# First blocks of a mixture of experts in plain fp32 for four experts, in place of split fp32r products for five

## The chip, the cores and the metric

The kernel runs on one core of one Trainium2 chip. Times are device microseconds (us) of whole executions; the profile is one further execution, with the start and end of the instructions on each engine: PE (TensorE matmuls) and PEld (its weight loads), DVE (VectorE), ACT (ScalarE), POOL (GpSimd) and SP, whose queue issues most of the DMAs.

## The reference

Attention over a window of 128 keys, for 8 batches, 8 heads, 576 positions and 64 columns a head; its output is a matrix x of 4608 tokens by 512. Then a mixture of 8 experts: each token goes to the best two by a noisy gate.

```python
logits = x @ w_gate
noise_scale = np.log1p(np.exp(x @ w_noise))
noisy_logits = logits + noise_scale * noise
top2 = np.argpartition(-noisy_logits, 2, axis=1)[:, :2]
...
for e in range(E):
    for k in range(2):
        mask = top2[:, k] == e
        ...
        h = np.maximum(x[mask] @ w1[e], 0.0)
        out[mask] += top2_w[mask, k, None] * (h @ w2[e])
```

w1[e] is 512 by 1024 and w2[e] 1024 by 512, so an expert is two chained products with a ReLU between them.

## The kernel before, in words

**Attention** runs over 32 pairs of heads, in three groups of query blocks each: scores (L455, and L448 for the last 64 positions, once a pair), softmax on DVE and ACT, transposes (L492), the product with the values (L523). For each batch of 576 tokens `rows` turns the result to token rows (L632, L635) and `gate` gets the logits (L655, L666); then `route(b)` chooses two experts for each token of batch b. `route` is a chain of some fifty small DVE operations with two stops on PE: counts over the tokens (L723 to L727, called R below) and the list of token numbers by expert (L770, called H below). `listed` (L777) takes the list from PSUM, and a POOL scatter (L843) adds it to `slots` in DRAM. Route b + 1 can't start its own chain before route b has gone through; the eight are numbered 0 to 7.

**First blocks.** When two batches are routed (`CUTS`), the first 256 tokens of each of the first NF = 5 experts are already known. Their experts' products (`first`, 5 blocks of 256 tokens) fill PE while attention goes on. A block has 8 steps f, one for every 128 of the 1024 inner columns. A step is `mm1` (L1086), which makes 128 inner columns for 256 tokens from four 128-row pieces of w1, then `middle` (ReLU, L1108 or L1110), then `mm2` (L1136), which adds to two 128 x 512 tiles of the output. The operands are fp32 numbers cut in a high and a low part of type fp32r, and each product is made as three: high by high, high by low, low by high. The low parts cost operations: for the weights a copy and a subtraction (`weight`, L960 to L962, the subtraction on POOL or DVE), for the tokens L1079, for the inner columns L1125. Tiles of this stage have names with `a`: `axh`, `axl`, `ahh`, `ahl`, `w1ha`, `w1la`, `w2ha`, `w2la`. Raw weights come into `raw1` and `raw2` (three buffers each), the parts into 5 sets (`wsets`).

**Second blocks.** When attention and all routes are over, `second_wave` gives the freed memory to new tiles (names with `b`), and all the other tokens go through the experts one after another, with f16 parts and again three products: blocks of 512 and 448 tokens for the experts that had a first block, of 512, 384 and 320 for the others (`BLOCKS`); CAP = 1216 tokens is the most of an expert that this takes. `mm2_flipped` (L1141) is the second product of an expert's last block. Tokens come by a POOL gather (L1034), are scaled (`fit`, L1051), transposed on PE (L1066) and split (L1076). `size_of_weights` reads the next expert's weights a second time (`mraw`) to find the scale of its f16 parts.

**Order.** The program is written by a small list scheduler (`Order`): each operation has a rank, and an engine that is free takes the ready operation of lowest rank, with durations that the code gives. What results is a fixed order for each engine, in which an instruction that waits holds up all behind it. `FFN0` and `FFN1` spread the ranks of the first blocks' steps; with fewer steps the distance between two steps grows. `named[0, NF - 1, 7]` is the point from which the second blocks' weights may be loaded.

## Time and profile before

| | |
|---|---|
| time, median of 3 runs | 1215.79 us (1214.66 to 1219.39) |
| the profiled execution | 1212.61 us |
| its span, from the first to the last instruction | 1210.7 us |
| mean granted TensorE clock | 0.988 |
| instructions | 20898 |

How to read it: busy times are sums of the spans of an engine's instructions, and the idle time in front of a group is put down to what ended it. Matmuls run in a pipeline, so one lasts longer than the distance to the next one; rates are read from the distance of their starts. The 40 slices of the page show three parts:

```profile
PE   7998899999997889999999999999999999999995
DVE  6798787788898897664664674584563473373310
POOL 5000121231255661320330331233033320332211
```

Each digit is the busy share of 30 us in tenths. PE is near its full share nearly everywhere; the dip in the 12th to 15th slice is the passage from attention to the second blocks, and there DVE and POOL are busiest.

### The profile page before, as it was taken

What the parts mean: (1) busy time and instruction counts of PE and PEld (TensorE: products, weight loads), DVE (VectorE), ACT (ScalarE), POOL (GpSimd) and SP (SyncE); (2) the same over time, 40 slices, a digit from 0 to 9 for tenths busy, and PEclk for the clock granted to TensorE, in tenths of its full rate; (3) what the DMA queues carried; (4) which work ended last, traced back from release to release, by engine and by line L of the source; (5) the groups of instructions that cost most, each with busy time, mean ns of one, the idle gap of its engine ahead of it and who ended that gap; (6) DMA issues with size and microseconds to landing.
All of it is one profiled execution on the core that took longest, in us unless ns stands there. A gap on an engine that the chain in (4) does not pass through costs nothing.

```text
span 1210.7 us, 20898 instructions
## 1 busy us (share of the span) xinstructions
PE 1142.3 (94%) x7336; PEld 690.1 (57%) x7336; DVE 775.9 (64%) x2483; ACT 547.3 (45%) x1378; POOL 310.7 (26%) x343
## 2 busy tenths in 40 slices
PE   7998899999997889999999999999999999999995
PEld 4666677777776764554544544545545654575552
DVE  6798787788898897664664674584563473373310
ACT  8776666667633353441432433342432441252311
POOL 5000121231255661320330331233033320332211
PEclk9999999999999999999999999999999999999998
DMA  8896545553267597562761862663663391352221
GB/s 289 281 319 208 172 130 172 161 151 125 77 184 179 125 280 217 134 186 91 178 187 45 206 171 54 186 191 58 193 166 62 80 264 41 62 114 45 35 27 23
DMA packets 138987, 177.57 MB, mean 147 GB/s; under 512 B 25728, under 2 KB 89472, under 8 KB 138880
## 3 DMA queue, kind: packets, MB, share of 16 engines
q1 hardware_dynamic: 120960, 135.87, 35.3%
q0 software_dynamic: 17920, 40.33, 17.5%
q8 instruction: 59, 0.97, 0.3%
q14 instruction: 48, 0.39, 0.1%
HBM read 134.76 MB, written 41.40 MB: 146 GB/s over the span
## 4 chain that ended last, share of the span: by engine, by line
PE 58%; DVE 13%; DMA 8%; issue 4%; POOL 1%; ACT 0%; SPq 0%; POOLq 0%; another core or an unknown queue 0%; DVEq 0%
PE bank L1086 23%; PE bank L1136 16%; PE bank L1141 8%; DMA mraw<-in_w_dram 5%; PE bank L523 2%; PE bank L492 2%; DMA xg<-xs_dram,ix 2%; DVE wam L988 2%; PE bank L1066 2%; PE bank L455 2%; DVE hot L765 1%; POOL out_dram L1215 1%; DVE bxl L1076 1%; DVE fit L1051 1%; DMA raw<-in_w_dram 1%
## 5 line engine op out<-in xcount | busy, mean ns | idle before, releaser
L1125 DVE SCALAR_TENSOR_TENSOR bhl<-bank,bhh 128x512 f16<-128x512 f32 (+3 forms) x152 | 93.9, 618 | 282.9 <-ACT bhh L1108 282.7
L1215 POOL DMA_INDIRECT out_dram<-yo,ix x70 | 110.3, 1575 | 534.3 <-ACT yo L245 480.4
L1108 ACT ACTIVATE bhh<-bank 128x512 f16<-128x512 f32 (+3 forms) x143 | 77.7, 543 | 332.8 <-PE bank L1086 331.9
L1086 PE MATMUL bank<-bxh,w1hb 128*128 128x512 f16 (+3 forms) x608 | 213.5, 351 | 0.0
L1086 PE MATMUL bank<-bxl,w1hb 128*128 128x512 f16 (+3 forms) x608 | 213.4, 351 | 0.0
L1086 PE MATMUL bank<-bxh,w1lb 128*128 128x512 f16 (+3 forms) x608 | 213.4, 351 | 0.0
L1086 PEld LDWEIGHTS <-w1hb 128*128 128x128 f16 x1216 | 118.0, 98 | 104.8 <-issue 1.9
L480 ACT ACTIVATE p<-p,nm 128x256 f32<-128x256 f32 (+2 forms) x288 | 133.8, 469 | 8.5 <-DVE nm L473 8.4
L1136 PE MATMUL bank<-w2hb,bhl 128*128 128x512 f16 (+1 forms) x352 | 133.5, 379 | 4.2 <-DVE bhl L1125 4.2
L1136 PE MATMUL bank<-w2hb,bhh 128*128 128x512 f16 (+1 forms) x352 | 133.7, 380 | 0.6 <-ACT bhh L1108 0.5
L1136 PE MATMUL bank<-w2lb,bhh 128*128 128x512 f16 (+1 forms) x352 | 133.4, 379 | 0.0
L1136 PEld LDWEIGHTS <-bhh 128*128 128x128 f16 (+1 forms) x704 | 67.3, 98 | 72.9 <-issue 4.6
L473 DVE CUSTOM_DVE_ANT_0 p<-bank,bias 128x256 f32<-128x256 f32 (+2 forms) x288 | 95.5, 380 | 17.4 <-PE bank L455 15.8
L1086 PEld LDWEIGHTS <-w1lb 128*128 128x128 f16 x608 | 59.5, 98 | 54.7
L962 POOL TENSOR_TENSOR w1la<-raw,w1ha 128x512 fp32r<-128x512 f32 x35 | 48.7, 1392 | 161.9 <-ACT w1ha L245 115.2
L523 PE MATMUL bank<-pT,vraw 128*64 128x128 f32 (+3 forms) x896 | 81.2, 303 | 5.6 <-ACT p L480 3.3
L492 PE MATMUL bank<-ident,p 128*128 128x128 f32 x512 | 83.2, 287 | 1.6 <-DVE pT L249 0.7
L1034 POOL DMA_INDIRECT xg<-xs_dram,ix x70 | 70.0, 1000 | 43.0 <-issue 37.9
L988 DVE TENSOR_REDUCE wam<-mraw 128x1 f32<-128x1024 f32 x56 | 67.7, 1211 | 19.9 <-DMA mraw<-in_w_dram 19.6
L455 PE MATMUL bank<-qk 64*128 64x256 f32 (+1 forms) x512 | 70.7, 389 | 10.2 <-DVE nm L473 5.3
L1141 PE MATMUL bank<-bhl,w2hb 128*128 128x448 f16 (+1 forms) x224 | 75.5, 337 | 0.0
L1141 PE MATMUL bank<-bhh,w2lb 128*128 128x448 f16 (+1 forms) x224 | 75.5, 337 | 0.0
(219 smaller groups left out, 2119.9 us busy)
## 6 DMA issues: line engine op xcount, KB each, us to landing
raw<-in_w_dram SPq DMA_DIRECT2D x208, 256.0 KB, 3.9
mraw<-in_w_dram SPq DMA_DIRECT2D x56, 512.0 KB, 6.6
qk<-in_qk_dram SPq DMA_DIRECT2D x32, 608.0 KB, 4.5
out_dram<-xg SPq DMA_DIRECT2D x10, 1024.0 KB, 8.6
vraw<-in_v_dram SPq DMA_DIRECT2D x16, 512.0 KB, 3.9
xs_dram<-x SPq DMA_DIRECT2D x32, 256.0 KB, 3.4
vraw<-in_v_dram SPq DMA_DIRECT2D x16, 128.0 KB, 5.5
xg<-xs_dram,ix POOLq DMA_INDIRECT x70, 4.8
```

The lines of the kernel that those rows point to most:

```text
L455: nc.tensor.matmul(s[h][:, o:o + c], qk[half, i * 128:i * 128 + 128], qk[half, QW + k0:QW + k0 + c], start=True, stop=True)
L473: nc.vector.tensor_tensor_reduce(out=p[:, z, h, 0:c], in0=s[h][:, o:o + c], in1=bv, scale=-0.125, scalar=3.0e38, op0=OP.add, op1=OP.min, a ...
L480: nc.scalar.activation(pv, pv, AF.Exp, bias=nm[:, z, h:h + 1], scale=-1.0, accum_out=den[:, z, 2 * g + h:2 * g + h + 1])
L492: nc.tensor.transpose(t[:, z], p[:, h, a:a + 128], ident)
L523: nc.tensor.matmul(o[half, o0:o0 + c], t[p0:128, kb, hh:hh + D], w, start=m == 0, stop=m == len(lst) - 1)
L988: yield dve(1.13, rank, lambda: nc.vector.tensor_reduce(o, t, axis=AX.X, op=OP.max, apply_absolute_value=True))
L1086: nc.tensor.matmul(t[:, 0:blk.n], wp[:, c], x[:, c, 0:blk.n], start=c == 0 and z == 0, stop=c == 3 and z == 2)
L1108: nc.scalar.activation(o, i, AF.Relu)
L1125: yield dve(0.07 + c * 0.00104, rank - MIDDLE, lambda: nc.vector.scalar_tensor_tensor(hl[:, 0:c], t[:, 0:c], 0.0, high, op0=OP.max, op1=OP ...
L1136: nc.tensor.matmul(blk.y[j][0:r], h[:, cs], wp, start=f == 0 and m == 0, stop=f == 7 and m == 2)
L1141: nc.tensor.matmul(blk.y[c][:, 0:blk.n], wp[:, c * 128:c * 128 + 128], h[:, 0:blk.n], start=f == 0 and m == 0, stop=f == 7 and m == 2)
L1215: ins = nc.gpsimd.indirect_dma_start(out=out, out_offset=bass.IndirectOffsetOnAxis(ap=blk.ix[0:r, j:j + 1], axis=0), in_=t[0:r], in_offset ...
```

## The change

The first blocks' products are made once, as fp32 matmuls on the raw weights and the raw tokens. The low parts of weights, tokens and inner columns, the copies and the subtractions that made them, and their tiles are gone; a weight is loaded straight into one of 8 sets (2 tiles each, not 4), and the three `hh` buffers were two. NF is 4: expert 4 has no first block, and its second blocks are those of 512, 384 and 320 tokens. The scheduler's durations for the two products are changed with them; the ranks' constants are as they were.

```diff
-NF = 5
+NF = 4
...
-    wsets = [Ring([weight_set(keep, F32R, f"a{z}") for z in range(5)]), Ring([])]
+    wsets = [Ring([(keep.tile([128, 4, 128], F32, name=f"w1a{z}"), keep.tile([128, DM], F32, name=f"w2a{z}"))
+                   for z in range(8)]), Ring([])]
...
-    rings1 = block_rings(keep, FIRST[0], F32R, "a", 2)
+    rings1 = block_rings(keep, FIRST[0], F32, "a", 3)
...
+                if p == 0:
+                    w = ev[2] = yield (wsets[p], r)
+                    mark(named[p, e, f])
+                    for z, src in enumerate((first_weight(e, f), second_weight(e, f))):
+                        spawn(weight(w[z], ev[z], r + 0.2 * z, src, e, z, f))
+                    continue
                 a = yield (raw1, r)
                 b = yield (raw2, r)
                 w = yield (wsets[p], r)
...
-    def weight(t, r, hi, lo, ev, rank, src, e, z, f):
+    def weight(t, ev, rank, src, e, z, f):
         yield from move(2.6e5, rank, lambda: nc.sync.dma_start(t, src))
-        yield either(0.52, 0.34, rank, LATE[5], lambda g: copy(g, hi, t))
-        yield Op((("POOL", 1.23, rank), ("DVE", 0.6, rank + WEIGHTS_LATE)),
-                 lambda g: engine[g].tensor_sub(lo, t, hi.bitcast(F32)))
-        put(r, t)
         mark(ev)
...
+        hi = blk.xh[:, :, cs]
+        yield either(0.48, 0.6, rank, LATE[6], lambda e: copy(e, hi, tv))
         if blk in second:
-            yield either(0.48, 0.6, rank, LATE[6], lambda e: copy(e, hi, tv))
-            yield dve(0.6, rank, lambda: nc.vector.tensor_sub(lo, tv, hi))
-        else:
-            yield either(0.48, 0.6, rank, LATE[6], lambda e: copy(e, hi, tv))
-            yield dve(0.6, rank, lambda: nc.vector.tensor_sub(lo, tv, hi.bitcast(F32)))
+            yield dve(0.6, rank, lambda: nc.vector.tensor_sub(blk.xl[:, :, cs], tv, hi))
...
     def mm1(blk, t, w, cc):
         for c in cc:
+            if blk not in second:
+                nc.tensor.matmul(t[:, 0:blk.n], w[0][:, c], blk.xh[:, c, 0:blk.n], start=c == 0, stop=c == 3)
+                continue
...
-            us = 3 * (blk.n / 2400 + (0.005 if p else 0.016))
+            us = 3 * (blk.n / 2400 + 0.005) if p else blk.n / 600
...
-        yield dve(0.07 + c * 0.00104, rank - MIDDLE, lambda: nc.vector.scalar_tensor_tensor(
-            hl[:, 0:c], t[:, 0:c], 0.0, high, op0=OP.max, op1=OP.subtract))
+        if blk in second:
+            yield dve(0.07 + c * 0.00104, rank - MIDDLE, lambda: nc.vector.scalar_tensor_tensor(
+                hl[:, 0:c], t[:, 0:c], 0.0, hh[:, 0:c], op0=OP.max, op1=OP.subtract))
...
     def mm2(blk, f, j, r, w):
         cs = slice(j * 128, j * 128 + r)
+        if blk not in second:
+            nc.tensor.matmul(blk.y[j][0:r], blk.h[f][1][0][:, cs], w[1], start=f == 0, stop=f == 7)
+            return
...
-                end = yield pe(0.655 if p else 0.69, rank, lambda: mm2(blk, f, j, r, ev[2]), False)
+                end = yield pe(0.655 if p else 0.86, rank, lambda: mm2(blk, f, j, r, ev[2]), False)
```

What this does to the order is seen in three places. First PE, right behind the last list H (route 7). Before, a step's products come in threes (`w1ha` and `w1la` are parts of one weight, `axh` and `axl` of the tokens; the number behind a name is the buffer):

```order
L1136 MATMUL bank_70<-w2ha_176,ahh_211 128x512
L1136 MATMUL bank_70<-w2la_177,ahh_211 128x512
L1136 MATMUL bank_70<-w2ha_176,ahl_213 128x512
L1136 MATMUL bank_72<-w2ha_176,ahh_211 128x512
L1136 MATMUL bank_72<-w2la_177,ahh_211 128x512
L1136 MATMUL bank_72<-w2ha_176,ahl_213 128x512
L1086 MATMUL bank_66<-axh_208,w1ha_178 128x256
L1086 MATMUL bank_66<-axl_210,w1ha_178 128x256
L1086 MATMUL bank_66<-axh_208,w1la_179 128x256
```

The changed kernel has at the same place (its L1085 is `mm1`, L1139 `mm2`, L1068 the transposes of the second blocks' tokens):

```order
L1139 MATMUL bank_70<-w2a_179,ahh_207 128x512
L1139 MATMUL bank_73<-w2a_179,ahh_207 128x512
L1085 MATMUL bank_67<-axh_204,w1a_180 128x256 x2
L1085 MATMUL bank_71<-axh_204,w1a_182 128x256
L1068 MATMUL bank_68<-ident,xg_121 128x128 x4
L1139 MATMUL bank_70<-w2a_181,ahh_205 128x512
L1139 MATMUL bank_73<-w2a_181,ahh_205 128x512
L1085 MATMUL bank_71<-axh_204,w1a_182 128x256 x3
```

One matmul stands for three. Counted over the whole order: when L448 comes for the 32nd and last time, 15 of 40 steps of `mm1` are behind it before, and 12.25 of 32 now; between the R of routes 6 and 7 there are 9.5 steps before and 4.25 now, between the last H and the first transpose of second tokens 6 and 4.75.

Second DVE, in route 7, from `u` (L710) to the largest logits (L715, MAX). Before:

```order
L710 TENSOR_SCALAR u<-y 128x40
L249 CAST w2ha_184<-raw_118 128x512
L247 TENSOR_SCALAR yo_206<-bank_68,gw_201 128x512
L782 SCALAR_TENSOR_TENSOR y<-u,y 128x40
L783 RECIPROCAL u<-u 128x40
L784 TENSOR_TENSOR y<-y,u 128x40
L785 TENSOR_TENSOR l<-l,y 128x40
L962 TENSOR_TENSOR w1la_183<-raw_115,w1ha_182 128x512
L787 SCALAR_TENSOR_TENSOR l<-lg_152,l 128x40
L788 TENSOR_TENSOR l<-l,noi 128x40
L789 TENSOR_TENSOR l<-l,lg_152 128x40
L1079 TENSOR_TENSOR axl_209<-bank_73,axh_207 128x4x128
```

Now (line numbers are lower by one there):

```order
L709 TENSOR_SCALAR u<-y 128x40
L781 SCALAR_TENSOR_TENSOR y<-u,y 128x40
L782 RECIPROCAL u<-u 128x40
L783 TENSOR_TENSOR y<-y,u 128x40
L784 TENSOR_TENSOR l<-l,y 128x40
L786 SCALAR_TENSOR_TENSOR l<-lg_152,l 128x40
L787 TENSOR_TENSOR l<-l,noi 128x40
L788 TENSOR_TENSOR l<-l,lg_152 128x40
L714 MAX tp<-l 128x8 x5
```

Everything that belonged to the first blocks has left the chain, and stays out of it to the end of route 7.

Third POOL, around the last scatter of a list. Before (L1317 is a small table, L1215 the scatter of a first block's output rows):

```order
L962 TENSOR_TENSOR w1la_183<-raw_117,w1ha_182 128x512
L962 TENSOR_TENSOR w1la_187<-raw_115,w1ha_186 128x512
L842 MEMSET pad 1x1
L843 DMA slots_dram<-listed,line_of_147 704x64
L1317 IOTA bias 1x80
L962 TENSOR_TENSOR w1la_191<-raw_116,w1ha_190 128x512
L962 TENSOR_TENSOR w2la_193<-raw_119,w2ha_192 128x512
```

Now, behind the same scatter (L842) and the table, up to the first gathers of second tokens (L1222 is the scatter of output rows, L1036 the gather):

```order
L1222 DMA out_dram<-yo_201,ids_172 5120x512
L1221 MEMSET pad 1x1
L1222 DMA out_dram<-yo_202,ids_172 5120x512
L1036 DMA xg_121<-xs_dram,ix_4062 128x520
L1036 DMA xg_122<-xs_dram,ix_4062 128x520
```

No subtraction is left on POOL; two scatters of a first block's output still stand between the last list and the first gather.

More of the change, by code (lines that the diff above doesn't have):

```diff
@@ L9 @@
 F32 = mybir.dt.float32
-F32R = mybir.dt.float32r
 F16 = mybir.dt.float16
@@ L898, in block_rings @@
     def block_rings(pool_, c, dt, name, hn):
-        return {"xh": ring(pool_, 2, [128, 4, c], dt, name + "xh"), "xl": ring(pool_, 2, [128, 4, c], dt, name + "xl"),
-                "hh": ring(pool_, hn, [128, c], dt, name + "hh"), "hl": ring(pool_, hn, [128, c], dt, name + "hl")}
-    wsets = [Ring([weight_set(keep, F32R, f"a{z}") for z in range(5)]), Ring([])]
+        return {r: ring(pool_, 2 if r[0] == "x" else hn, [128, 4, c] if r[0] == "x" else [128, c], dt, name + r)
+                for r in (("xh", "hh") if dt == F32 else ("xh", "xl", "hh", "hl"))}
+    wsets = [Ring([(keep.tile([128, 4, 128], F32, name=f"w1a{z}"), keep.tile([128, DM], F32, name=f"w2a{z}"))
+                   for z in range(8)]), Ring([])]
     wam = keep.tile([128, 2, 2, 8], F32, name="wam")
@@ L946, in weights @@
                 for z, (t, rg, src) in enumerate(((a, raw1, first_weight(e, f)), (b, raw2, second_weight(e, f)))):
-                    make = weight if p == 0 else scaled_weight
-                    spawn(make(t, rg, w[2 * z], w[2 * z + 1], ev[z], r + 0.2 * z, src, e, z, f))
+                    spawn(scaled_weight(t, rg, w[2 * z], w[2 * z + 1], ev[z], r + 0.2 * z, src, e, z, f))
     def first_weight(e, f):
@@ L966, in weight @@
             yield dve(0.6, rank + SIZES[0], lambda: nc.vector.tensor_reduce(
-                wam[:, e % 2, z, f:f + 1], hi.bitcast(F32), axis=AX.XY if z == 0 else AX.X, op=OP.max,
-                apply_absolute_value=True))
+                wam[:, e % 2, z, f:f + 1], t, axis=AX.XY if z == 0 else AX.X, op=OP.max, apply_absolute_value=True))
             mark(seen[e, f])
@@ L1030, in tokens @@
         blk.xh = yield (blk.rings["xh"], rank)
-        blk.xl = yield (blk.rings["xl"], rank)
+        if blk in second:
+            blk.xl = yield (blk.rings["xl"], rank)
         for j, r in blk.tiles:
@@ L1072, in turn_tokens @@
         mark(blk.weighed)
-        hi, lo = blk.xh[:, :, cs], blk.xl[:, :, cs]
+        hi = blk.xh[:, :, cs]
+        yield either(0.48, 0.6, rank, LATE[6], lambda e: copy(e, hi, tv))
         if blk in second:
-            yield either(0.48, 0.6, rank, LATE[6], lambda e: copy(e, hi, tv))
-            yield dve(0.6, rank, lambda: nc.vector.tensor_sub(lo, tv, hi))
-        else:
-            yield either(0.48, 0.6, rank, LATE[6], lambda e: copy(e, hi, tv))
-            yield dve(0.6, rank, lambda: nc.vector.tensor_sub(lo, tv, hi.bitcast(F32)))
+            yield dve(0.6, rank, lambda: nc.vector.tensor_sub(blk.xl[:, :, cs], tv, hi))
         put(tb, a)
@@ L1116, in middle @@
             put(blk.rings["xh"], blk.xh)
-            put(blk.rings["xl"], blk.xl)
+            if blk in second:
+                put(blk.rings["xl"], blk.xl)
         hh = yield (blk.rings["hh"], rank)
         blk.h[f][1].append(hh)
-        hl = yield (blk.rings["hl"], rank)
-        blk.h[f][1].append(hl)
+        if blk in second:
+            hl = yield (blk.rings["hl"], rank)
+            blk.h[f][1].append(hl)
         yield either(0.052 + c * 0.000833, 0.067 + c * 0.00104, rank - MIDDLE, LATE[8], lambda e: relu(
             e, hh[:, 0:c], t[:, 0:c]))
-        high = hh[:, 0:c] if blk in second else hh[:, 0:c].bitcast(F32)
-        yield dve(0.07 + c * 0.00104, rank - MIDDLE, lambda: nc.vector.scalar_tensor_tensor(
-            hl[:, 0:c], t[:, 0:c], 0.0, high, op0=OP.max, op1=OP.subtract))
+        if blk in second:
+            yield dve(0.07 + c * 0.00104, rank - MIDDLE, lambda: nc.vector.scalar_tensor_tensor(
+                hl[:, 0:c], t[:, 0:c], 0.0, hh[:, 0:c], op0=OP.max, op1=OP.subtract))
         put(hbr, t)
```

## The prediction

> **What bounds the kernel now.** I read the engines' shares first, then busy time by stage, then what PE waited for at the passage between the stages.
>
> ```profile
> PE 1142.3 (94%) x7336; PEld 690.1 (57%) x7336; DVE 775.9 (64%) x2483; ACT 547.3 (45%) x1378; POOL 310.7 (26%) x343
> ```
>
> PE is busy in 94% of the span. So the first question is what the change does to PE's own work, the second where PE's idle time lies. Busy time by stage (start and end, length, then PE, PEld, DVE, ACT, POOL):
>
> ```profile
> 0.00:141.30 141.30, 123.89 (x1110) 86.81 (x1110) 114.21 (x528) 103.54 (x372) 22.65 (x41) 0.98 0.79 261
> 141.30:325.00 183.70, 179.78 (x1574) 132.15 (x1573) 150.49 (x677) 127.26 (x446) 39.92 (x36) 1.00 0.45 138
> 325.00:444.30 119.30, 99.92 (x718) 83.82 (x718) 107.61 (x305) 48.88 (x111) 66.38 (x62) 0.96 0.65 174
> 444.30:1199.00 754.70, 738.68 (x3942) 387.28 (x3941) 403.63 (x976) 267.61 (x453) 178.68 (x202) 1.00 0.49 124
> ```
>
> PE idles 17.4 us before the first block's first product (141.3), 3.9 us up to the last pair's L448 (325), 19.4 us in the passage to the first second-block product (444.3), and 16.0 us in all the rest. Attention and the second blocks are PE's; only the passage has something to win, and there DVE is busy 107.6 of 119.3 us. What PE waited for in it, longest first:
>
> ```profile
> PE bank L1136 <- DVE ahl L1125: 13.3, 6, 5.1
> ```
>
> 13.3 of the 19.4 us go by waiting for the low part of the inner columns, which the change removes.
>
> **PE's work in the first blocks.** The pace of the split products, from their starts:
>
> ```profile
> 397.14 0.39 PE L1136 MATMUL bank<-w2la,ahh 128*128 128x512 f32 x1
> ...
> 399.66 0.28 PE L1086 MATMUL bank<-axh,w1ha 128*128 128x256 f32 x1
> ...
> 402.53 0.40 PE L1136 MATMUL bank<-w2ha,ahh 128*128 128x512 f32 x1
> ```
>
> From 397.14 to 399.66 lie 11 matmuls of 512 columns (0.229 us each), from there to 402.53 lie 24 of 256 (0.120). A step is 12 x 0.120 + 6 x 0.229 = 2.81 us; 40 steps make 112.4 us.
>
> No full fp32 matmul of 256 or 512 columns stands in the trace. The nearest is L448, with 192 columns on the whole array; beside it stand f16 matmuls of known width and a narrower fp32 one (mean ns behind the bar and the busy time):
>
> ```profile
> L448 PE MATMUL bank<-qk x64: 323/326/524, 11.2 to 325.0; 128*128 128x192 f32 x64
> ```
>
> ```profile
> L1136 PE MATMUL bank<-w2hb,bhh 128*128 128x512 f16 x344 | 130.5, 379 | 0.6 <-ACT bhh L1108 0.5
> L1086 PE MATMUL bank<-bxh,w1hb 128*128 128x384 f16 x96 | 31.3, 326 | 0.0
> L655 PE MATMUL bank<-xu,wgn 128*32 128x256 f32 x128 | 10.6, 404 | 0.7 <-DVE x L635 0.7
> ```
>
> ```profile
> 480.24 2.59 PE bank L1136 x12
> ```
>
> L448 runs 32 times and leaves 64 records, so an fp32 matmul is two passes; each lasts 326 ns, as an f16 matmul of 384 columns does. A pass thus takes as long as f16 with twice the columns. A pass of 256 columns then has the pace of f16 with 512: 2.59 / 12 = 0.216 us; one of 512 takes twice that. A step becomes 4 x 2 x 0.216 + 2 x 2 x 0.432 = 3.46 us, 32 steps 110.6 us: **1.8 us less** on PE in all. The upper end comes from L655, whose pass of 256 columns lasts 404 ns, not 379: 25 ns on 16 such pieces is 0.4 us a step, 12.8 us in all. The lower end is L448's shortest, 323 against 326: nothing. I take 3.46, since L448 uses the whole array as the new products do, and L655 a quarter of it.
>
> **The passage.** How much of this falls behind 325 us? The order has 15 of 40 steps ahead of the last L448 before, 12.25 of 32 now, so PE's filling of attention is 42.2 us before and 42.4 now: attention should end where it did. There remain 25 steps before (the 100 products of this kind in that stage, four a step) and 19.75 now.
>
> ```profile
> L1086 PE MATMUL bank<-axh,w1ha 128*128 128x256 f32 x100 | 30.0, 300 | 0.0
> ```
>
> Of the 99.9 busy us, 25 x 2.81 = 70.3 are steps. Some were slow after a wait:
>
> ```profile
> 390.29 0.80 PE L1136 MATMUL bank<-w2ha,ahl 128*128 128x512 f32 x1 [5.12 <-DVE ahl L1125]
> ```
>
> ```profile
> 394.29 0.39 PE L1136 MATMUL bank<-w2ha,ahl 128*128 128x512 f32 x1
> ```
>
> Nine matmuls in 4.00 us, where 9 x 0.229 = 2.1 would do: 1.9 us. The other 27.7 are token and row transposes, gates and lists, which stay. Now 19.75 x 3.46 = 68.3 + 27.7 = 96.0 us, so with PE never idle the second blocks begin at 325 + 96.0 = 421.0.
>
> Does DVE let it? Its route chain, which the passage waits for, holds three long stalls. First an ordinary L789, then the same in route 7 and what POOL did, then another:
>
> ```profile
> 351.85 0.19 DVE L789 TENSOR_TENSOR l<-l,lg 128x40 f32<-128x40 f32 x1
> ```
>
> ```profile
> 381.32 6.16 DVE L789 TENSOR_TENSOR l<-l,lg 128x40 f32<-128x40 f32 x1
> ```
>
> ```profile
> 381.85 1.88 POOL L962 TENSOR_TENSOR w2la<-raw,w2ha 128x512 fp32r<-128x512 f32 x1
> ```
>
> ```profile
> 385.58 1.83 POOL L962 TENSOR_TENSOR w1la<-raw,w1ha 128x512 fp32r<-128x512 f32 x1
> ```
>
> ```profile
> 410.06 4.87 DVE L1298 TENSOR_SCALAR bias<-bias 1x8 int32<-1x8 int32 x1
> ```
>
> L789 lost 6.0 us and ended (387.5) with the last of four POOL subtractions in a row. L1298, on eight numbers, took 4.9. POOL has no subtraction left, so both go. [...]
>
> The period of a route is seen from the list of route 6 to that of route 7, with DVE's first-block operations between them (busy us behind the bar, then idle time before them):
>
> ```profile
> 372.01 0.21 DVE L777 TENSOR_SCALAR listed<-bank 80x64 f32<-80x64 f32 x1
> ```
>
> ```profile
> 408.90 0.21 DVE L777 TENSOR_SCALAR listed<-bank 80x64 f32<-80x64 f32 x1
> ```
>
> ```profile
> L1125 DVE SCALAR_TENSOR_TENSOR ahl<-bank,ahh 128x256 fp32r<-128x256 f32 x8 | 3.3, 417 | 5.6 <-ACT ahh L1108 5.6
> L962 DVE TENSOR_TENSOR w2la<-raw,w2ha 128x512 fp32r<-128x512 f32 x4 | 2.7, 682 | 0.0
> L962 DVE TENSOR_TENSOR w1la<-raw,w1ha 128x512 fp32r<-128x512 f32 x3 | 2.0, 683 | 0.0
> L1079 DVE TENSOR_TENSOR axl<-bank,axh 128x512 fp32r<-128x512 f32 x2 | 1.4, 678 | 0.0
> L249 DVE CAST w1ha<-raw 128x512 fp32r<-128x512 f32 x2 | 0.8, 418 | 0.0
> ```
>
> 36.9 us, less 6.0 of stall, 5.6 of waiting for ACT and 10.2 of these operations, leaves **15.1 us** for a route alone. PE has 4.25 steps between the two R now, 14.7 us, and about 1 us of R and H besides: the two are level, and I give 1 us of idle PE to each of routes 6 and 7. Behind the last list:
>
> ```profile
> 409.64 1.44 POOL L843 DMA_INDIRECT slots_dram<-listed,line_of  x1 [3.19 <-DVE listed L778]
> ```
>
> ```profile
> 421.10 0.14 DVE L885 SCALAR_TENSOR_TENSOR ix<-list,spare 128x4 f32<-128x4 f32 x1
> ```
>
> ```profile
> 430.66 0.60 PE L1066 MATMUL bank<-ident,xg 128*128 128x128 f32 x4
> ```
>
> From the list's scatter to the first second token on PE it took 21.0 us; without the 4.7 of L1298 that is 16.3, and PE has 4.75 steps, 16.4 us, to fill it. The gather stands behind two output scatters on POOL that wait for their own block, so I give it 2 us. **Idle left: 4 us.** The second blocks begin at 425.0, 19.3 us earlier. What is late next is PE itself.
>
> **The second blocks.** Expert 4 now takes 1216 tokens, not 960. The last flipped product of experts 3 to 6:
>
> ```profile
> 789.56 0.35 PE L1141 MATMUL bank<-bhl,w2hb 128*128 128x448 f16 x1
> ```
>
> ```profile
> 875.02 0.35 PE L1141 MATMUL bank<-bhl,w2hb 128*128 128x448 f16 x1
> ```
>
> ```profile
> 980.90 0.30 PE L1141 MATMUL bank<-bhl,w2hb 128*128 128x320 f16 x1
> ```
>
> ```profile
> 1089.89 0.30 PE L1141 MATMUL bank<-bhl,w2hb 128*128 128x320 f16 x1
> ```
>
> Experts 4, 5 and 6 take 85.5, 105.9 and 109.0 us. Now expert 4 is what 5 was (long, behind a short one), and 5 what 6 was: 105.9 + 109.0 + 109.0 less the three is **23.5 us more**. By matmuls alone, 256 columns in 192 at 0.108 us are 20.7, the low end.
>
> **Costed at nothing:** the conversions gone from ACT, DVE and POOL before 325 us (PE is busy 179.8 of 183.7 us there), and the weights. SP's order loads 16 pieces of weights, not 10, ahead of the sixth pair's queries. PE waited for such a load once, at the start:
>
> ```profile
> PE bank L455 <- DMA qk<-in_qk_dram: 4.8, 1, 4.8
> ```
>
> If four pairs loaded ahead don't cover the six pieces, that wait could come again: 0 to 4.8 us; I take 0.
>
> **The sum:** -19.3 + 23.5 = +4.2 us. An end of attention 1 or 2 us earlier is likely, with fewer and longer bursts of first-block matmuls between its own (74 for 90), so I put it at **+3 us**: 1215.6 for the profiled execution's 1212.61. The median of the runs, 1215.79, lies 3.2 above that execution; against it the forecast is 1218.8.
>
> **The rivals.** (a) Slower by far: the passage stays paced by waits. The ReLU of a step sits on ACT behind conversions of second weights that wait for their loads, and a step's `mm2` holds up all of PE. Against: PE has two matmuls (0.86 us) between; for: the 5.6 us for which DVE waited on ACT's ReLU above. If a route takes 21 us, not 15 (it decides from 15.7), two routes cost 12 us more, and a ReLU wait like the 5.1 of before makes 17: +20, 1236 by the median.
> (b) Faster: DVE and ACT, rid of the parts, also close gaps of attention. Up to 325 us PE idles 21.3 us, 4.8 of them in the one load wait; if half of the other 16.5 goes and the passage has no idle left, it is 3 - 8 - 4 = -9: 1207. Against: before 141 us there are few first-block operations to be rid of.
> (c) The weight load shows. Each pass loads 128 fp32 columns:
>
> ```profile
> L448 PEld LDWEIGHTS bank<-qk x64: 186/190/332, 11.0 to 324.8; 128*128 128x128 f32 x64
> ```
>
> Twelve loads of 0.19 us a step, none hidden, are 73 us in 32 steps: 1292. [...]
> (d) The change is what it says but an fp32 pass costs as L655: +12.8, 1232.
>
> **How the numbers follow.** Forecast 0.45, (a) 0.30, (b) 0.17, (c) 0.03, (d) 0.05. A measurement of this kernel tells about 0.5% (6 us) from no change. Faster by more: (b) and a little of the forecast's edge, 0.20; slower: (a), (c), (d), less (a)'s mild cases, 0.36; the same: 0.44. The range reaches to (a) and (b): 1205 to 1236.
>
> **What would show it.** Right: starts of `mm1` passes 0.216 us apart; the last L448 (L447 there) at 325; no DVE operation of the route over 2 us; the first second-block product at 425; expert 4 taking 106. Wrong: passes at 0.24 or more; PE waiting for ACT's ReLU or for the routes in the passage by over 10 us; L447 many us off 325.

## The result, and the profile after

The changed kernel takes 1194.55 us (median of 4 runs, 1193.53 to 1195.78) against 1215.22 for the kernel before: a ratio of 0.9839, with an interval of 0.9816 to 0.9863. The profiled execution took 1195.78 us, with a span of 1193.9 and a mean clock of 0.996 (before: 1212.61, 1210.7 and 0.988). It is faster by 1.6%, where +3 us was forecast and 1205 was the lower end of the range.

The page's engine totals and three of its 40-slice rows, for the changed kernel:

```profile
PE 1146.1 (96%) x7164; PEld 666.6 (56%) x7164; DVE 712.7 (60%) x2422; ACT 518.4 (43%) x1317; POOL 223.9 (19%) x280
...
PE   7999999999998999999999999999999999999995
...
DVE  7898867787866846646646746733843573372310
...
POOL 1000100010023113203303312322303320232211
```

PE's share rose from 94 to 96%; its sum hardly moved (1142.3 to 1146.1). The dip in PE's 12th to 15th slice has become one slice of 8, and POOL's early part is nearly empty. Busy time by stage (columns as in the prediction; the stages end at the first block's first product, at the last pair's L447 and at the first second-block product):

```profile
0.00:145.50 145.50, 131.05 (x1202) 92.13 (x1203) 122.16 (x587) 109.90 (x401) 10.14 (x32) 1.00 0.82 275
145.50:313.20 167.70, 167.45 (x1361) 111.60 (x1360) 122.90 (x595) 106.34 (x382) 9.75 (x12) 1.00 0.45 135
313.20:402.80 89.60, 86.59 (x490) 57.58 (x489) 65.86 (x267) 32.74 (x76) 20.97 (x25) 1.00 0.69 196
402.80:1181.00 778.20, 760.79 (x4118) 405.34 (x4116) 401.74 (x977) 268.59 (x459) 178.62 (x207) 1.00 0.47 119
```

Two rows with the first and last start of a group stand for the stages' ends:

```profile
L447 PE MATMUL bank<-qk x64: 326/326/528, 11.1 to 313.2; 128*128 128x192 f32 x64
```

```profile
L1088 PE MATMUL bank<-bxh,w1hb x640: 299/352/390, 402.8 to 1177.8; 128*128 128x512 f16 x64, 128*128 128x448 f16 x32, 128*128 128x384 f16 x32, 128*128 128x320 f16 x32
```

The last L447 starts at 313.2 (before, L448 at 325.0; forecast 325), the first second-block product at 402.8 (444.3; forecast 425). PE now idles 14.4 us up to 145.5, 0.3 up to the last pair and 3.0 in the passage, 17.7 in all where it was 40.7; and the granted clock, third column from the end, is 1.00 in every stage where it was 0.98 and 0.96 in two.

The pace of the new products, from the starts on PE in the passage (start, us, instruction), and the route's addition that had lasted 6.16 us (L789 before), with shortest, median and longest in ns:

```profile
350.06 1.89 PE L1085 MATMUL bank<-axh,w1a 128*128 128x256 f32 x8
351.79 0.59 PE L1139 MATMUL bank<-w2a,ahh 128*128 128x512 f32 x1
```

```profile
L788 DVE TENSOR_TENSOR l<-l,lg x8: 187/196/200, 67.9 to 357.7; 128x40 f32<-128x40 f32 x8
```

Eight passes of 256 columns in 1.73 us are 0.216 us each, as forecast, and the stalls of the route are gone. So the price of a pass was right; the sum was wrong all the same.

### The profile page after: what moved, and what is told of

Read it like the earlier page. It is cut to its first block, busy times and chain, and to the rows that moved or that the text cites. A ratio compares the mean times of both kernels' runs of the same rounds, so it can differ in the third digit from the quotient of the medians.

```text
span 1193.9 us, 20221 instructions
## 1 busy us (share of the span) xinstructions
PE 1146.1 (96%) x7164; PEld 666.6 (56%) x7164; DVE 712.7 (60%) x2422; ACT 518.4 (43%) x1317; POOL 223.9 (19%) x280
## 3 DMA queue, kind: packets, MB, share of 16 engines
q0 software_dynamic: 17920, 40.33, 17.6%
## 4 chain that ended last, share of the span: by engine, by line
PE 79%; DVE 7%; DMA 7%; issue 4%; ACT 1%; POOL 1%; SPq 0%; POOLq 0%; another core or an unknown queue 0%; DVEq 0%; ACTq 0%
PE bank L1088 24%; PE bank L1143 17%; PE bank L1148 7%; PE bank L522 5%; PE bank L491 5%; DMA mraw<-in_w_dram 5%; PE bank L454 5%; PE bank L1085 4%; PE bank L1139 4%; PE bank L1068 2%; DVE wam L989 2%; PE bank L631 2%; PE bank L654 1%; DVE p L472 1%; PE bank L447 1%
## 5 line engine op out<-in xcount | busy, mean ns | idle before, releaser
L1088 PE MATMUL bank<-bxh,w1hb 128*128 128x512 f16 (+3 forms) x640 | 222.2, 347 | 0.0
L1088 PE MATMUL bank<-bxl,w1hb 128*128 128x512 f16 (+3 forms) x640 | 222.1, 347 | 0.0
L1088 PE MATMUL bank<-bxh,w1lb 128*128 128x512 f16 (+3 forms) x640 | 222.1, 347 | 0.0
L1222 POOL DMA_INDIRECT out_dram<-yo,ix x72 | 113.2, 1572 | 562.4 <-ACT yo L244 484.7
L1088 PEld LDWEIGHTS <-w1hb 128*128 128x128 f16 x1280 | 124.4, 98 | 106.1 <-issue 2.2
L1143 PE MATMUL bank<-w2hb,bhl 128*128 128x512 f16 (+1 forms) x376 | 142.6, 379 | 6.9 <-DVE bhl L1129 6.9
L1143 PE MATMUL bank<-w2hb,bhh 128*128 128x512 f16 (+1 forms) x376 | 142.8, 380 | 0.5 <-ACT bhh L1110 0.5
L1143 PE MATMUL bank<-w2lb,bhh 128*128 128x512 f16 (+1 forms) x376 | 142.5, 379 | 0.0
L1143 PEld LDWEIGHTS <-bhh 128*128 128x128 f16 (+1 forms) x752 | 72.0, 98 | 78.5 <-issue 4.6
L1036 POOL DMA_INDIRECT xg<-xs_dram,ix x72 | 70.7, 981 | 44.3 <-issue 18.5
L454 PE MATMUL bank<-qk 64*128 64x256 f32 (+1 forms) x512 | 68.3, 383 | 8.6 <-DMA qk<-in_qk_dram 4.7
L522 PEld LDWEIGHTS bank<-pT,vraw 128*64 128x64 f32 (+1 forms) x896 | 51.2, 136 | 41.6 <-issue 7.7
L1148 PE MATMUL bank<-bhl,w2hb 128*128 128x448 f16 (+1 forms) x224 | 73.8, 330 | 0.0
L1148 PE MATMUL bank<-bhh,w2hb 128*128 128x448 f16 (+1 forms) x224 | 73.8, 330 | 0.0
```

Source lines behind the costliest of these rows:

```text
L454: nc.tensor.matmul(s[h][:, o:o + c], qk[half, i * 128:i * 128 + 128], qk[half, QW + k0:QW + k0 + c], start=True, stop=True)
L522: nc.tensor.matmul(o[half, o0:o0 + c], t[p0:128, kb, hh:hh + D], w, start=m == 0, stop=m == len(lst) - 1)
L1088: nc.tensor.matmul(t[:, 0:blk.n], wp[:, c], x[:, c, 0:blk.n], start=c == 0 and z == 0, stop=c == 3 and z == 2)
L1143: nc.tensor.matmul(blk.y[j][0:r], h[:, cs], wp, start=f == 0 and m == 0, stop=f == 7 and m == 2)
L1148: nc.tensor.matmul(blk.y[c][:, 0:blk.n], wp[:, c * 128:c * 128 + 128], h[:, 0:blk.n], start=f == 0 and m == 0, stop=f == 7 and m == 2)
L1222: ins = nc.gpsimd.indirect_dma_start(out=out, out_offset=bass.IndirectOffsetOnAxis(ap=blk.ix[0:r, j:j + 1], axis=0), in_=t[0:r], in_offset ...
```

## Where the time went

To price the steps in place, I add for every PE instruction the time from its start to the next start, less the wait that the timeline shows in brackets. By that, up to the first second-block product:

| us | before | after | moved | forecast |
|---|---|---|---|---|
| PE waits | 39.8 | 17.1 | -22.7 | -15.4 |
| PE busy at half clock, the half that is lost | 7.0 | 0.0 | -7.0 | -1.9 |
| PE's work at full clock | 397.5 | 385.7 | -11.8 | -2.0 |
| first second-block product at | 444.3 | 402.8 | -41.5 | -19.3 |
| from there to the end | | | +24.9 | +23.5 |

The first three rows are the step of the prediction that failed, split in its parts. The last row holds 1.7 us of the last first-block step, whose `mm2` the changed kernel runs behind that point: 23.2 us are the second blocks' own.

**Work at full clock.** The first blocks' steps take 131.4 us before (3.28 each of 40, half clock included) and 116.1 after (3.63 each of 32; 114.4 of it ahead of the first second-block product). The pure pace gives 2.81 and 3.46. Where the 0.47 us that a split step costs beyond its pace come from is seen at the edges of a burst, here in attention (PE, timeline of the kernel before):

```profile
207.88 0.36 PE L1086 MATMUL bank<-axh,w1ha 128*128 128x256 f32 x1
208.09 0.28 PE L1086 MATMUL bank<-axl,w1ha 128*128 128x256 f32 x1
208.20 0.29 PE L1086 MATMUL bank<-axh,w1la 128*128 128x256 f32 x1
208.33 0.60 PE L492 MATMUL bank<-ident,p 128*128 128x128 f32 x4
208.68 0.36 PE L1086 MATMUL bank<-axh,w1ha 128*128 128x256 f32 x1
...
209.00 0.29 PE L1086 MATMUL bank<-axh,w1la 128*128 128x256 f32 x1
209.22 0.49 PE L455 MATMUL bank<-qk 64*128 64x256 f32 x2
```

Three matmuls should take 0.36 us; the first burst takes 0.45, the second 0.54, with no wait shown. The first matmul of a burst takes 0.21 to the second, which in the middle of a burst is 0.12. In the changed kernel, at the same place, a burst of six and its neighbours:

```profile
204.84 1.46 PE L1085 MATMUL bank<-axh,w1a 128*128 128x256 f32 x6
206.23 1.09 PE L522 MATMUL bank<-pT,vraw 128*64 128x256 f32 x12
```

1.39 us for 6 x 0.216 = 1.30. Over attention, the bursts take 50.8 us for 40.8 of pure pace before (63 bursts, 0.16 us beyond each) and 45.7 for 41.7 after (54 bursts, 0.07).

The steps are not the whole of it. Everything else that PE does up to the last pair, nearly the same instructions, took 250.3 us at full clock before and 253.7 after. So PE's work in attention fell by 1.7 us in all, not by the 5.1 of the steps: part of what is counted here at the edges of the split bursts may sit at the edges of their neighbours after the change.

**Half clock.** Windows of one us of the kernel before (length, then the engines' busy us, PE first; the granted clock is the third column from the end):

```profile
107.00:108.00 1.00, 0.68 (x4) 0.30 (x2) 1.00 (x7) 1.00 (x5) 0.00 (x0) 1.00 0.00 0
108.00:109.00 1.00, 0.69 (x8) 0.57 (x8) 0.90 (x7) 1.00 (x6) 0.00 (x0) 1.00 0.60 73
109.00:110.00 1.00, 0.76 (x8) 0.42 (x4) 0.91 (x6) 0.53 (x3) 0.00 (x0) 1.00 0.66 248
110.00:111.00 1.00, 0.29 (x4) 0.29 (x6) 0.96 (x5) 0.31 (x1) 0.00 (x0) 0.98 0.96 321
111.00:112.00 1.00, 1.00 (x8) 0.44 (x5) 0.97 (x5) 0.72 (x3) 0.00 (x0) 0.50 0.21 15
...
114.00:115.00 1.00, 1.00 (x12) 0.42 (x4) 0.00 (x0) 0.52 (x3) 0.00 (x0) 0.81 0.00 0
```

The clock is halved for 3.4 us (0.04 + 3 x 1.0 + 0.38 by these rows), and PE is busy in nearly all of it, so 1.7 us go. Such stretches of 3.4 us, or two in a row, stand behind PE's waits at 22, 110, 387 (two) and 431 us: 17.1 us at half clock, of which PE was busy 14, which is 7.0 us lost. The changed kernel has none before its second blocks. In the four us ahead of the drop at 111.0 PE's longest gap is 0.94 us, and PE is busy 60% of them.

## The experiments

In the table that closes this section all kernels stand side by side. Ratios are to the kernel before on the same chip.

**e1_nolow** is the kernel before, five blocks and three fp32r products each, without making the low parts: the products read the high parts in their place.

```diff
-        yield Op((("POOL", 1.23, rank), ("DVE", 0.6, rank + WEIGHTS_LATE)),
-                 lambda g: engine[g].tensor_sub(lo, t, hi.bitcast(F32)))
...
-            yield dve(0.6, rank, lambda: nc.vector.tensor_sub(lo, tv, hi.bitcast(F32)))
...
-        yield dve(0.07 + c * 0.00104, rank - MIDDLE, lambda: nc.vector.scalar_tensor_tensor(
-            hl[:, 0:c], t[:, 0:c], 0.0, high, op0=OP.max, op1=OP.subtract))
+        if blk in second:
+            yield dve(0.07 + c * 0.00104, rank - MIDDLE, lambda: nc.vector.scalar_tensor_tensor(
+                hl[:, 0:c], t[:, 0:c], 0.0, hh[:, 0:c], op0=OP.max, op1=OP.subtract))
...
```

> The kernel before with five experts and three fp32r products, but no low parts are made for the first blocks: the three products all take the high parts (so the low terms of the first blocks' products are left out). PE runs the same instructions; the subtractions on POOL and DVE and the 40 L1125 of this stage are gone. Theory 1, the relief of DVE and POOL ends PE's waits: PE's idle time up to the first second-block product falls from 40 us to 17 or less, that product starts at 416 to 424 instead of 444, time 1188 to 1196. Theory 2, the edges of PE's bursts (19 us above the pace inside a burst) are short waits for DVE's low parts that the profile counts as busy: then they go too, the product starts at 400 to 408, time 1172 to 1180. Rival, the cheap product on PE is what pays: nothing here, 1211 to 1218.

Measured 1185.42 us, ratio 0.9756 (0.9725 to 0.9787). Its two stages up to the second blocks:

```profile
0.00:324.24 324.24, 305.88 (x2707) 221.80 (x2708) 254.36 (x1198) 229.07 (x810) 21.92 (x46) 0.99 0.62 196
324.24:415.70 91.46, 88.59 (x684) 77.18 (x682) 68.47 (x282) 44.60 (x99) 24.21 (x29) 1.00 0.80 226
```

Without any cheaper product, the relief of DVE and POOL alone brings the second blocks to 415.7: the passage has 2.9 us of idle PE instead of 19.4. PE's waits up to there, 20.1 us, are 3 more than the first theory allowed, and the time is 3 us below its range. The attention part ends where it did (324), so the 11.8 us that the changed kernel wins there need more than this relief. The steps still cost 3.2 us each: the edges are no wait for DVE.

**e2_plain5** and **e3_split4** do one half of the change each: plain products for five experts, split products for four.

```diff
-NF = 4
+NF = 5
```

```diff
-NF = 5
+NF = 4
```

> The changed kernel with a first block for expert 4 again (NF = 5). If PE is the limit of all stages, the first stage grows by 8 steps of 3.46 us and two token tiles, 28 to 30 us, and the second falls by 24 to 25: 1197 to 1200 against the changed kernel's 1194.5. Rival, four experts for five cost what the prediction said (+23.5 against little in the first stage): 1172 to 1185.

> The kernel before with a first block for four experts only (NF = 4), split products as before. If a split step costs PE 3.3 us with its edges: first stage -26 us and some 4 us of idle less, second +25: 1207 to 1213. Rival, the number of experts makes the whole gain: 1193 to 1197. Rival, a split step costs 2.81 us as in the prediction: -22.5 + 25 and the same idle, 1216 to 1220.

Plain products for five: 1201.12 us, ratio 0.9899 (0.9876 to 0.9922), 1 us over what was expected. Split products for four: 1221.02, ratio 1.0077 (1.0042 to 1.0112), above all that was expected. What PE waited for up to the second blocks, and the passage, in e3_split4:

```profile
PE bank L1136 <- DVE ahl L1125: 12.0, 9, 2.7
```

```profile
321.90:429.10 107.20, 82.96 (x610) 67.17 (x609) 95.92 (x292) 44.87 (x98) 53.68 (x51) 0.92 0.64 171
```

Eight steps less, and PE idles 24.2 of 107.2 us there: with split products the other engines set the length of the passage, and work taken from PE turns into waits. So a block less costs 8 us in the split kernel and wins 4 to 7 in the plain one (0.9899 against 0.9867 and 0.9839). The two halves don't add up: fewer blocks pay only with plain products, while plain products pay alone (0.9899).

**e4_pool** and **e7_poolw** put work on POOL in the changed kernel, behind each first-block weight, whose result nobody uses: one subtraction, which reads SBUF, or three memsets, which only write it.

```diff
...
+        tv = t.rearrange("p a b -> p (a b)") if z == 0 else t
+        yield pool(1.23, rank, lambda: nc.gpsimd.tensor_sub(junk, tv, tv))
```

```diff
...
+        yield pool(1.23, rank, lambda: [nc.gpsimd.memset(junk, 0.0) for _ in range(3)])
```

> The changed kernel, and on GpSimd 64 subtractions of 128x512 fp32 from SBUF (one behind the load of each first-block weight, result unused, nobody waits for it): the reads of SBUF that the old subtractions made, without their use. Theory (GpSimd's reading held up the route's DVE operations, and its end is part of what the passage won): route operations of over 2 us come back (one L789 took 6.16 us before, none is over 0.2 in the changed kernel), the first second-block product comes 4 to 12 us later than 402.8, the time rises by 4 to 12 us. Rival (the stalls were hidden beside PE's work): operations of DVE stall, but the first second-block product stays within 3 us of 402.8 and the time within 3 us.

> The changed kernel, and on GpSimd 192 memsets of 128x512 fp32 (three behind the load of each first-block weight, some 0.5 us each), which write SBUF and read nothing. Theory 1 (it is GpSimd's reading that holds up a DVE operation with two SBUF inputs): the route's L788 stays near 0.19 us and the time within 3 us of the changed kernel, though GpSimd is as busy as with the subtractions. [...]

With the subtractions 1209.84 us, ratio 0.9963 (0.9947 to 0.9979); with the memsets 1200.84, ratio 0.9898 (0.9874 to 0.9921). PE, DVE, ACT and SP have the same instructions in the same order in both, so the 9 us between them come with POOL's subtractions, which read SBUF where the memsets only write it. Three groups of the route on DVE up to 411 us, and POOL's own, first with subtractions, then with memsets:

```profile
L764 DVE TENSOR_SCALAR hot<-steps,d,numbers 128x64 f16<-128x64 f16 x80 | 24.3, 361 | 0.0
L783 DVE TENSOR_TENSOR y<-y,u 128x40 f32<-128x40 f32 x8 | 3.5, 434 | 0.2
L751 DVE TENSOR_TENSOR tmp<-mine,line 80x8 f32<-80x8 f32 x7 | 3.0, 434 | 0.0
L969 POOL TENSOR_TENSOR junk<-w2a 128x512 f32<-128x512 f32 x32 | 34.5, 1078 | 30.9 <-DMA w2a<-in_w_dram 29.9
```

```profile
L764 DVE TENSOR_SCALAR hot<-steps,d,numbers 128x64 f16<-128x64 f16 x80 | 19.1, 346 | 0.0
L783 DVE TENSOR_TENSOR y<-y,u 128x40 f32<-128x40 f32 x8 | 1.6, 198 | 0.2
L751 DVE TENSOR_TENSOR tmp<-mine,line 80x8 f32<-80x8 f32 x7 | 1.0, 148 | 0.0
L968 POOL MEMSET junk<- 128x512 f32 x192 | 105.4, 549 | 10.3
```

With 105 us of memsets L751 and L783 are as short as in the changed kernel (164 and 196 ns there), with 69 us of subtractions (34.5 and as much for `w1a`) more than twice as long. The memsets lengthen others, each with one tensor in: L745 and L746 take 314 and 323 ns, where they take 185 and 172 with the subtractions and 180 and 176 in the changed kernel. In all, the route's operations (L709 to L806) are 91 us of DVE in the changed kernel, 98 with the memsets and 110 with the subtractions; of the 12 us between the two the three groups above have 9.1. L788, on which the expectation was set, lost only 0.9, and the longest operation was another, an L751 of 2.16 us. That it is the reading in a subtraction which does this, as both expectations have it, fits L751 and L783; no run changes the reading alone. What the 9 us consist of on PE is in the table: 3.5 us more waits, and 6.1 more lost to half clock behind those waits. The memsets' kernel, too, is 4 to 7 us slower than the changed one; the scheduler put its steps in other places (13 ahead of the last pair, not 12.25), and the cause of that part is open.

**e5_ahl** and **e10_copies** bring back one other piece of side work each: the inner columns' low part on DVE, and the weights' copies on ACT or DVE.

```diff
...
-        if blk in second:
-            yield dve(0.07 + c * 0.00104, rank - MIDDLE, lambda: nc.vector.scalar_tensor_tensor(
-                hl[:, 0:c], t[:, 0:c], 0.0, hh[:, 0:c], op0=OP.max, op1=OP.subtract))
+        low = hl if blk in second else junk
+        yield dve(0.07 + c * 0.00104, rank - MIDDLE, lambda: nc.vector.scalar_tensor_tensor(
+            low[:, 0:c], t[:, 0:c], 0.0, hh[:, 0:c], op0=OP.max, op1=OP.subtract))
```

```diff
...
+        tv = t.rearrange("p a b -> p (a b)") if z == 0 else t
+        yield either(0.52, 0.34, rank, LATE[5], lambda g: copy(g, junk[g], tv))
```

> The changed kernel, and on DVE the old low part of the inner columns (one operation of 128x256 behind each ReLU, 32 of 0.41 us), made into a tile that no product reads, but before which the step's second product may not start. Theory (the wait for the low part was a large part of PE's idle time in the passage): PE waits behind it again, 5 to 12 us more idle time before the first second-block product, which comes at 408 to 415; the time rises by 5 to 12 us. Rival (without the other conversions DVE is free enough to make it in time, so that the wait was a symptom of the loaded DVE): under 3 us in both.

> The changed kernel, and behind each load of a first-block weight the old copy of 128x512 on ACT or DVE (64 in all, into a tile that nobody reads), behind which alone the weight may be used. Theory (no single one of the old operations paced the passage, their sum did): under 3 us more idle time of PE before the second blocks and a time within 5 us of the changed kernel. Rival (the copies on ACT stood ahead of the ReLU and made the steps wait): PE waits for ACT's ReLU by over 5 us and the time rises by over 6 us.

With the low part: 1200.42 us, ratio 0.9892 (0.9869 to 0.9915), second blocks at 404.9, PE waits 16.1. With the copies: 1203.04, ratio 0.9918 (0.9896 to 0.9939), second blocks at 410.2, waits 19.4. Neither adds more than some 2 us to PE's waits; the wait for `ahl` that headed the prediction (13.3 us) does not return with `ahl` itself. It was a sign of a loaded DVE. The time of e5_ahl lies 3 to 6 us above the changed kernel's in two other sessions, which is little more than these differ. The copies' kernel is 6.4 us slower than e8_again on the same chip, so the theory's 5 us were a little short; it lost 5.1 us to half clock, and PE's waits ahead of `mm2` were 2.1 us, so that the rival, which named the ReLU, had the time and not its cause.

**e6_plain3** takes one more block away.

```diff
-NF = 4
+NF = 3
```

> The changed kernel with first blocks for three experts (NF = 3): 8 steps less before the second blocks, 256 tokens more in them. If PE's work alone set the start of the second blocks, they would start 28.6 us earlier (8 steps of 3.575 us), and with 24.9 us more behind it the time falls by some 4 us. If the chain of routes, list and gather sets it (the order has the last of the 24 steps done before the second tokens arrive), PE idles 8 to 14 us in the passage: the start comes 15 to 21 us earlier, and the time is 1198 to 1206.

Measured 1216.68 us, ratio 1.0022 (1.0006 to 1.0038), above both expectations. The second blocks start at 401.0, 1.8 us earlier than with four blocks. PE's largest wait in the passage:

```profile
PE bank L1068 <- DVE w1lb L1024: 12.1, 1, 12.1
```

With 24 steps PE is through before the second blocks' first tokens and weights are ready, and most of the block taken away turns into waits (38.7 us in all, 21 more than with four). Four plain blocks fill the passage, three don't.

**e8_again** is the changed kernel, unedited, on the chip of the next three.

> The changed kernel itself, on the chip of the next three kernels, so that they are compared with it and not with a run on another chip: a ratio of 0.981 to 0.987 to the kernel before.

1196.67 us, ratio 0.9867 (0.9848 to 0.9887), against 0.9839 on the first chip: a difference of 3 us between two chips' sessions says how far ratios of different sessions may be compared.

**e9_one** is e1_nolow with one fp32r product of the three.

```diff
...
+            if blk not in second:
+                nc.tensor.matmul(t[:, 0:blk.n], w[0][:, c], blk.xh[:, c, 0:blk.n], start=c == 0, stop=c == 3)
+                continue
...
+        if blk not in second:
+            nc.tensor.matmul(blk.y[j][0:r], hh[:, cs], w[2], start=f == 0, stop=f == 7)
+            return
```

> The kernel before without low parts (as in e1_nolow, same order), and of the three fp32r products of the first blocks only one is made, high by high. What it tells is how a split step's cost beyond 2.81 us (3.16 in e1_nolow) arises. Theory (each burst of fp32r products among the fp32 work of attention pays at its edges, whatever its length): 40 steps cost 40 x 0.94 = 37.6 us of pure products plus the same 13.8 us of edges, 49 to 53 us in all. Rival (every fp32r matmul runs 12% longer there than in the burst that was read): 40 x 0.94 x 1.12 = 42 us. PE should idle much more, as the steps no longer fill it; the time itself tells little.

All 40 steps take 69.8 us up to the second blocks, over either number: PE, with little to do, waits 52 us, and runs 43 us at half clock. The part of attention, where the clock is 0.99, does tell the two apart. There 15.75 steps are 14.4 us of pure pace and take 28.2: 13.8 us beyond, in 67 bursts of 1.4 matmuls each, 0.21 a burst. In e1_nolow the same place has 10.5 us beyond, in 67 bursts of 4.1 matmuls, 0.16 a burst. A cost in proportion to the products would have been 3.5 us. The cost is one of edges, nearly the same with 1.4 matmuls in a burst as with 4.1. The time was 1169.72 us, ratio 0.9647 (0.9627 to 0.9667).

**e11_all** brings all of the side work back into the changed kernel, unused: copies, the weights' subtractions on POOL or DVE, both kinds of low parts.

```diff
...
+        yield either(0.52, 0.34, rank, LATE[5], lambda g: copy(g, junk[g], tv))
+        yield Op((("POOL", 1.23, rank), ("DVE", 0.6, rank + WEIGHTS_LATE)),
+                 lambda g: engine[g].tensor_sub(junk[g], tv, tv))
...
+        low = blk.xl[:, :, cs] if blk in second else junk["DVE"].rearrange("p (c n) -> p c n", c=4)[:, :, 0:r]
+        yield dve(0.6, rank, lambda: nc.vector.tensor_sub(low, tv, hi))
...
+        low = hl if blk in second else junk["DVE"]
+        yield dve(0.07 + c * 0.00104, rank - MIDDLE, lambda: nc.vector.scalar_tensor_tensor(
+            low[:, 0:c], t[:, 0:c], 0.0, hh[:, 0:c], op0=OP.max, op1=OP.subtract))
```

> The changed kernel with all of the old side work back and unused: the weights' copies, the weights' subtractions on GpSimd or DVE, the tokens' and the inner columns' low parts on DVE (behind each of which its product waits, as before), while the products stay plain fp32 for four experts and the tiles as in the changed kernel. Theory (the gain is DVE's, ACT's and GpSimd's relief, not cheaper products): PE idles 38 to 50 us up to the first second-block product, as in e3_split4 (47), which comes at 425 to 440, and the time is 1212 to 1226. Rival (the products, the eight sets of weights and the third buffer of inner columns make the gain): idle under 25 us and a time under 1203.

1209.82 us, ratio 0.9973 (0.9960 to 0.9986): 13 of the 16.5 us that the change won on that chip are gone (e8_again 1196.67, the kernel before 1213.21). The start of the second blocks, 418.8, PE's waits, 26.2, and the time fall between the two expectations. Its passage:

```profile
320.40:418.80 98.40, 92.03 (x472) 60.14 (x472) 84.48 (x284) 43.80 (x91) 38.90 (x42) 0.98 0.62 171
```

Of the 15.6 us by which the second blocks start later than in e8_again, 8.6 are waits, 1.4 half clock, and 5.6 PE's work at full clock: 1.7 of it is the last `mm2`, which stands ahead of that point here, and most of the rest is longer work outside the steps, for a reason that is open. PE idles 6.4 us in this passage, and 24.2 in that of e3_split4, which has four blocks and the same kinds of side work too, with split products: 1221.02 us against 1209.82, on the same chip in another session. So the side work alone doesn't make e3_split4 slow. POOL has also less to do here: 38.9 us of work in this passage, against 53.7 in that of e3_split4.

**e12_tight** and **e13_split4_hh3** ask whether the buffers had a part: the changed kernel with the old five sets and two `hh`, and e3_split4 with a third `hh` and `hl`.

```diff
-                   for z in range(8)]), Ring([])]
+                   for z in range(5)]), Ring([])]
...
-    rings1 = block_rings(keep, FIRST[0], F32, "a", 3)
+    rings1 = block_rings(keep, FIRST[0], F32, "a", 2)
```

```diff
-NF = 5
+NF = 4
...
-    rings1 = block_rings(keep, FIRST[0], F32R, "a", 2)
+    rings1 = block_rings(keep, FIRST[0], F32R, "a", 3)
```

> The changed kernel with the old numbers of buffers: five sets of weights, not eight, and two buffers of inner columns, not three. Theory (the gain is the other engines' relief; the buffers take no part): within 4 us of the changed kernel (ratio 0.982 to 0.990), the first second-block product at 400 to 407, PE idle under 21 us before it. Rival (loads further ahead and a third buffer are what keeps PE fed): PE waits for weights or for the ReLU, 24 us or more idle, a ratio of 0.991 or more.

> The kernel before with first blocks for four experts (as e3_split4, 1.0077) and a third buffer of the high and of the low inner columns. Theory (the side work paces the passage): as e3_split4, ratio 1.003 to 1.011, PE idle 40 us or more before the second blocks, most of it behind DVE. Rival (the third buffer lets the steps run ahead of DVE): idle under 32 us, ratio under 0.998.

1193.69 us, ratio 0.9839 (0.9820 to 0.9858), and 1222.67, ratio 1.0080 (1.0054 to 1.0107): the one as the changed kernel, the other as e3_split4. Neither the third `hh` nor the eight sets of the changed kernel had a part in its time.

All of them side by side: the ratio, the start of the second blocks, and of the time up to there PE's waits and what PE lost to half clock (us, from one profile each):

| kernel | ratio | second blocks at | PE waits | half clock |
|---|---|---|---|---|
| before | 1 | 444.3 | 39.8 | 7.0 |
| changed | 0.9839 | 402.8 | 17.1 | 0.0 |
| e8_again (changed) | 0.9867 | 403.2 | 17.6 | 0.0 |
| e12_tight | 0.9839 | 403.3 | 17.1 | 0.0 |
| e5_ahl | 0.9892 | 404.9 | 16.1 | 1.7 |
| e7_poolw | 0.9898 | 410.7 | 21.4 | 1.7 |
| e10_copies | 0.9918 | 410.2 | 19.4 | 5.1 |
| e4_pool | 0.9963 | 421.6 | 24.9 | 7.8 |
| e11_all | 0.9973 | 418.8 | 26.2 | 1.4 |
| e6_plain3 | 1.0022 | 401.0 | 38.7 | 2.6 |
| e2_plain5 | 0.9899 | 434.0 | 17.7 | 0.0 |
| e1_nolow | 0.9756 | 415.7 | 20.1 | 1.7 |
| e3_split4 | 1.0077 | 429.1 | 47.9 | 5.5 |
| e13_split4_hh3 | 1.0080 | 428.4 | 48.0 | 5.1 |
| e9_one | 0.9647 | 396.4 | 52.2 | 16.1 |

## Why the prediction was wrong

**What held.** A pass of 256 columns takes 0.216 us. From their first product on, the second blocks cost 24.9 us more, 23.2 without the last first-block `mm2` (23.5 forecast); expert 4 took 105.6 (106 forecast; from 750.64 to 856.27, the last flipped products, L1148, of experts 3 and 4). No route operation on DVE is over 2 us: L788 takes 0.19 to 0.20, and L1305, which was L1298, 0.17. Before, L1298 had ended at 414.93, just behind the third of three POOL subtractions in a row (L962, from 413.30 for 1.60 us). PE idles 3.0 us in the passage (4 forecast). No weight load shows: loads of 0.19 us each (L1085, PEld) go with passes that start 0.216 apart, as loads of 0.19 did before with split products that started 0.120 apart. So rival (c) falls, and with passes of 0.216 so does (d). Rival (a), a passage paced by waits, did not come; rival (b), waits closing in attention as well, had the right sign and named -8 us for attention and -4 for the passage, of which 6.7 and 1.0 beyond the forecast came.

**The price of a split step.** "A step is 12 x 0.120 + 6 x 0.229 = 2.81 us; 40 steps make 112.4 us" is the step that failed most. It read the pace in the middle of a long burst in the passage, and took it for all 40 steps, of which 15 stand in attention in bursts of a few matmuls between fp32 work. In place, a step took 3.28 us; the plain step, put at 3.46, took 3.63. The same prediction counted bursts in attention (90 and 74 by the order; 63 and 54 show in the timeline) and gave them 1 or 2 us in all; their edges were worth 10 us in attention alone, and 4 in the changed kernel. "1.8 us less" on PE was 15.3 (131.4 to 116.1), 3.7 of it half clock; some 2 us went the other way in PE's other work.

**"Attention should end where it did."** It ended 11.8 us earlier: 6.7 us of waits, 3.4 lost to half clock before, and 1.7 of work (the steps 5.1 less, 50.8 us to 45.7; all else 3.4 more). The waits were costed at nothing because PE was busy 179.8 of 183.7 us in the stage up to 325; but most of them lay in the stage ahead of it, of which the prediction said nothing, except in rival (b). PE waits in the whole of attention went from 20.7 to 14.0.

**"The other 27.7 ... stay."** What was left of the passage's busy time beyond pure steps was taken for transposes, gates and lists. Part of it was edges and half clock: the steps there took 80.6 us where 70.3 of pure pace was taken off, and now 68.7, without the last `mm2` of 1.7, where 68.3 was put in. So 96.0 us of work was 86.6.

**The clock.** The one slow stretch that was priced (1.9 us) was one of four; all four went with the waits that they followed. That is 7.0 us, so a wait that such a stretch follows costs more than its own length: at 110 us a gap of 0.94 us, and 1.7 us lost to the clock behind it.

**The cause.** The gain doesn't come from cheaper products: at four blocks the plain ones cost PE 116.1 us against 106.5 in e3_split4. That the other engines' relief is enough for it is shown: e1_nolow wins 27 us by relief alone (its output lacks the low terms), and e11_all loses 13 of 16.5 us without it. POOL's subtractions are the largest single piece found (9 us between e4_pool and e7_poolw). But relief is not all that the change does: e11_all, with its side work, is still 11 us below e3_split4, and PE waits 26.2 us where it waited 47.9. Fewer and longer matmuls, weights that go straight into their sets, another order of the scheduler, or less work on POOL may make that difference; no run tells them apart. Why a burst of fp32r among fp32 work costs 0.16 us at its edges, and one of fp32 0.07, was not settled.

## What to carry to other kernels

The pace inside a long burst is a lower end (2.81 us a split step here, 3.28 in place): price a piece of filling work where it stands, by the distance from the instruction before it to the one behind it, and count its bursts. When work of an engine off the critical path goes, look at every stage for waits that it caused, not at the stage with most of them, and add the clock that PE loses behind each wait (7.0 us here). When two halves of a change act on the two sides of one balance, as blocks on PE and side work on DVE here, test all four corners: one half alone (e3_split4) was slower than before, the other faster.

## What the hardware showed that was not expected

- In the kernel before, half clock came in stretches of 3.4 us, one of them double, and not behind long gaps alone: 0.94 us was the longest one ahead of the stretch at 111 us, where PE was busy 60% of four us.
- 69 us of POOL subtractions, read by nobody, cost the program 9 us more than 105 us of POOL memsets.
- A burst of fp32r products between fp32 matmuls took 0.21 us beyond its pace with 1.4 matmuls in it (e9_one), and 0.16 with 4.1 (e1_nolow).
- An fp32 matmul on the whole array was two passes here, of 0.216 us each for 256 columns and 0.43 for 512 (L1139: two from 351.79 to 352.65); f16 with 512 columns took 0.216. The weight loads, of 128 columns and 0.19 us each, don't show.
